# Sixteen slots instead of fourteen in an attention unit, and one VectorE operation less in the filler's gelu

## The chip, the cores and the metric

The kernel runs on one core of a Trainium2 chip. The metric is the device time of one execution in microseconds (us), median of three runs. A core has five engines with in-order queues of their own: TensorE (PE, with its weight loads listed as PEld), VectorE (DVE), ScalarE (ACT), GpSimd (POOL) and SyncE (SP), which issues the DMAs here.

## The reference

One transformer block in parallel form on x of 2048 tokens by 640 channels, float32:

```
xn = layernorm(x)
q, k, v = split(xn @ wqkv)              # 32 heads of 20 channels
s = (q k^T) / sqrt(20), kept where 0 <= i - j < 256, else -1e9
A = (softmax(s) @ v) @ wo               # sliding-window attention
B = (gelu_tanh(xn @ w_gate) * (xn @ w_up)) @ w_down     # 1728 hidden channels
out = x + A + B
```

The gelu is the tanh approximation: 0.5 g (1 + tanh(sqrt(2/pi) (g + 0.044715 g^3))).

## The kernel before

**Precision.** The dense products run in float32r with every operand split into a high and a low part (xh, xl for the normalized x; wqh, wql and so on for weights). A dense block of 128 rows by 512 tokens is then 3 x 5 = 15 matmuls: three combinations of parts, five slices of the 640 channels (dense_steps, L82). Queries and keys are stored as three bf16 parts in HBM and loaded as a stack, so that one matmul of 120 rows gives scores of float32 quality.

**Stages.** From 0 to 64 us: layernorm, transposes, first projections. From 64 to 714 us: the attention stage, into which the rest of the q, k and v projections and the gate and up products of eight of the fourteen column blocks of the gated layer are woven. From 714 us on: the remaining gate and up products, then w_down and wo and the sum.

**The attention stage.** A *unit* is one group of four heads and one chunk of 512 queries: 8 groups x 4 chunks = 32 units (NU). What a unit needs:

- 16 *maxima* (max_piece, L410 and L412): for one head and one block of 128 queries the scores against up to 384 keys, one or two bf16 matmuls into a bank of ps_m, and one VectorE operation that adds the mask and takes the row maximum. Chunk 0 has narrower ones (128, 256, 384, 384 columns). There are three ps_m banks (psm, L109). When a unit's sixteenth maximum is queued, two VectorE operations (L417, L418) negate the maxima and split them in two bf16 parts (nm).
- max_end (L424 to L427): one matmul turns nm around into ps_n, which takes a bank of the same three; ACT copies it (mr), a DMA puts it as two more rows under the queries' stack. With them the scores of the second pass come out less their maximum.
- 12 *exponentials* (exp_piece, L462 and L464): bf16 matmuls over 122 rows into one of two banks of ps_e, then Exp on ACT into the tile P; behind every fourth of them GpSimd cuts the diagonal (L470, L473).
- av_unit (L484): P times v in float32, 32 or 48 short matmuls into ps_o, a copy (ob) and DMAs.

The maxima run ahead of the exponentials: 24 of them are done before unit 0 starts, so while unit u takes its exponentials, maxima 8 to 15 of unit u+1 and 0 to 7 of unit u+2 are taken.

**Slots.** The order on TensorE, ACT and VectorE is the program's order (manual_schedule). attention() lays a unit out in NS = 14 *slots*. Slot 0 first takes av_unit of the unit before. Every even slot is a *cluster*: in slots 0 to 10 two exponentials, then two maxima, three of them in slots 6 and 12. After that every slot pulls RATE/NS = 3.54 matmuls from *filler()*, a generator over the dense work (ps_d, ps_v; ps_v counts 0.65). A max_end is due MXD = 4 slots after the slot of its sixteenth maximum.

Work that follows a dense block is not queued at once: defer(n, fn) puts it n slots later, and tick() at a slot's head queues what is due, ahead of that slot's exponentials and maxima. gate_up_fill has the chain c1 (ACT: copy gs and Square, L528, L529), c2 (VectorE, L534 and L535), c3 (ACT: Tanh, L539), c4 (VectorE, L543), one slot apart, and c5 (VectorE, L550, and a store to HBM) a slot after the up product. A q or k block has upper (ACT conversion L215, VectorE difference r L216) and lower (ACT conversion L203, GpSimd, DMAs). The split of the next weights puts a conversion on ACT (L510). x_sums queues 80 VectorE additions (L613, eight sets of ten, two slots apart, the first at slot XS0, sets XSN slots apart) for a later stage. The second half of v is projected when the slot number has reached V1_SLOT.

load_stack (L390) issues the six DMAs of a unit's queries and keys two units ahead, at slot 0.

Before unit 0 there is a ramp of twelve steps, each with two single maxima and 4 filler matmuls behind each, and then GAP = 16 of filler.

Of the kernel before, what the change touches and what calls it, by code (L numbers as in the profile page):

```python
# [12 lines left out]
AF = mybir.ActivationFunctionType  # L13
OP = mybir.AluOpType
# [12 lines left out]
SCALE = 1.0 / math.sqrt(DH)  # L27
NEG = -3.0e38
QROWS = 122
NS = 14  # L30
RATE = 49.6
V1_SLOT = 169
MXD = 4
NFA = 8
NDA = 2
WARM = 64
XS0, XSN = 24, 50
RAMP = 4.0
GAP = 16
VW = 1408  # L40
# [5 lines left out]
def block_kernel(ctx, tc, x, xt, wqk, wv, wo, wgu, wd, wdl, out):  # L46
    nc = tc.nc
# [30 lines left out]
    def dense_steps(ps, wh, wl, rh, rl, nk, cost=1.0):  # L78
        n = 0
        for a, b in ((wh, rh), (wl, rh), (wh, rl)):  # L80
            for k in range(nk):
                nc.tensor.matmul(ps, a(k), b(k), start=n == 0, stop=n == 3 * nk - 1)  # L82
                n += 1
                yield cost
# [84 lines left out]
    now = [None]  # L169

    def at(slot, fn, *a):
        acts.setdefault(slot, []).append((fn, a))

    def defer(n, fn, *a):
        if now[0] is None:
            fn(*a)
        else:
            at(now[0] + n, fn, *a)
# [94 lines left out]
    def run(*gens):  # L273
        for gen in gens:
            for _ in gen:
                pass
# [105 lines left out]
    def load_stack(u):  # L382
        g, c = divmod(u, NC)
        for m in range(80 * g // 128, (80 * g + 79) // 128 + 1):
            assert (m, c) in done and (m + 5, c) in done, (u, m)

        for dst, src, parts in ((qs[u % NQ], qd[c], (0, 1, 2)), (ks[u % NK], kd[c], (0, 0, 0))):
            slot = 0
            for part, n in zip(parts, (3, 2, 1)):
                nc.sync.dma_start(dst[DH * slot:DH * (slot + n)].rearrange("p j t -> p (j t)"),  # L390
                                  src[g, part:part + n].rearrange("s (d j) t -> (s d) (j t)", j=4))
                slot += n
# [3 lines left out]
    def max_piece(u, i):  # L396
        g, c = divmod(u, NC)
        j, b = divmod(i, 4)
        q, k = qs[u % NQ], ks[u % NK]
        if i == 0:  # L400
            maxes[u] = ap.tile([128, 4, 4], F32, name="mx", tag="mx")
        ps = psm.tile([128, 384], F32, name="ps_m", tag="mx")
        lh = q[0:120, j, 128 * b:128 * b + 128]
        old = max(0, 256 - 128 * b) if c else 0
        n0 = max(0, 128 * b - 256)
        n = old + 128 * b + 128 - n0
        parts = [(0, old, ks[(u - 1) % NK][0:120, j, C - old:C])] if old else []
        parts.append((old, n, k[0:120, j, n0:128 * b + 128]))
        for lo, hi, rhs in sorted(parts, key=lambda p: p[1] - p[0]):
            nc.tensor.matmul(ps[:, lo:hi], lh, rhs, start=True, stop=True)  # L410
        junk = ap.tile([128, 384], BF, name="junk", tag="junk", bufs=1)
        nc.vector.tensor_tensor_reduce(out=junk[:, 0:n], in0=ps[:, 0:n], in1=mask[:, 384 - n:384], scale=1.0,  # L412
                                       scalar=NEG, op0=OP.add, op1=OP.max, accum_out=maxes[u][:, j, b:b + 1])
        if i == 15:
            mx = maxes.pop(u)
            nm = nms[u % 2]
            nc.vector.tensor_scalar(nm[:, 0, 0], mx, -1.0, None, op0=OP.mult)  # L417
            nc.vector.scalar_tensor_tensor(nm[:, 0, 1], mx, -1.0, nm[:, 0, 0], op0=OP.mult, op1=OP.subtract)  # L418
            maxes[u] = nm
# [85 lines left out]
    def split_later(pool, bufs, raw):  # L505
        hi = pool.tile([128, KT, 128], F32R, name="wqh", tag="wqh", bufs=bufs)
        lo = pool.tile([128, KT, 128], F32R, name="wql", tag="wql", bufs=bufs)

        def high():
            nc.scalar.activation(hi, raw, AF.Copy)  # L510
            for k in range(KT):
                defer(1 + k, low, k)

        def low(k):
            nc.gpsimd.tensor_tensor(out=lo[:, k], in0=raw[:, k], in1=hi[:, k].bitcast(F32), op=OP.subtract)  # L515

        defer(1, high)
        return hi, lo

    def gate_up_fill(f, ws, c):  # L520
        cs = slice(c * C, (c + 1) * C)
        pss = []
        st = {}

        def c1():
            gs = st["g"] = hp.tile([128, C], F32, name="gs", tag="gs")
            t = st["t"] = hp.tile([128, C], F32, name="he", tag="he", bufs=2)
            nc.scalar.activation(gs, pss[0], AF.Copy)  # L528
            nc.scalar.activation(t, pss[0], AF.Square)  # L529
            defer(1, c2)  # L530

        def c2():
            gs, t = st["g"], st["t"]
            nc.vector.tensor_scalar(t, t, 0.044715, 1.0, op0=OP.mult, op1=OP.add)  # L534
            nc.vector.tensor_tensor(out=t, in0=gs, in1=t, op=OP.mult)  # L535
            defer(1, c3)

        def c3():
            nc.scalar.activation(st["t"], st["t"], AF.Tanh, scale=math.sqrt(2.0 / math.pi))  # L539
            defer(1, c4)  # L540

        def c4():
            nc.vector.scalar_tensor_tensor(st["g"], st["t"], 1.0, st["g"], op0=OP.add, op1=OP.mult)  # L543
            st["done"] = True

        def c5():
            if "done" not in st:
                defer(1, c5)
                return
            nc.vector.scalar_tensor_tensor(st["t"], st["g"], 0.5, pss[1], op0=OP.mult, op1=OP.mult)  # L550
            nc.sync.dma_start(hd[f][c], st["t"])

        for i, (wh, wl) in enumerate(ws):
            ps = psd.tile([128, C], F32, name="ps_d", tag="dn")
            pss.append(ps)
            yield from dense_steps(ps, lambda k: wh[:, k, :], lambda k: wl[:, k, :],
                                   lambda k: xh[:, k, cs], lambda k: xl[:, k, cs], KT)
            defer(1, c5 if i else c1)
# [6 lines left out]
    def filler():  # L565
# [6 lines left out]
        for s, (kind, i) in enumerate(sets[:-1]):  # L572
            nxt = []
            after = sets[s + 1]
            for c in range(NC):
# [14 lines left out]
                if c in (1, 2) and c <= len(raws):  # L590
                    nxt.append(split_later(*pools[(s + 1) % 2], raws[c - 1]))
                if pending and now[0] >= V1_SLOT:
                    pending = False
# [65 lines left out]
    def pull_max(n, slot):  # L659
        for _ in range(n):  # L660
            x = next(stream, None)
            if x is None:
                return
            max_piece(*x)
            if x[1] == 15:
                at(slot + MXD, max_end, x[0])

    def tick():
        return [y for t in sorted(t for t in acts if t <= now[0]) for y in acts.pop(t)]

    def pull_fill(n):
        debt[0] += n
        while debt[0] > 0:
            debt[0] -= next(fill, 1.0)

    def attention():
        now[0] = -1
        load_stack(0)
        load_stack(1)
        load_stack(2)  # L680
        for i, (p, k, half) in enumerate((p, k, half) for p in range(NC // 2) for k in range(2) for half in range(2)):
            for j, fn in enumerate(x_sums(p, k, half)):
                at(XS0 + XSN * i + 2 * j, fn)
        for i in range(12):
            now[0] = i - 13
            for fn, a in tick():
                fn(*a)
            for _ in range(2):
                pull_max(1, now[0])
                pull_fill(RAMP)  # L690
        pull_fill(GAP)
        for u in range(NU + 1):
            if 1 <= u and u + 2 < NU:
                load_stack(u + 2)
            for i in range(NS):
                T = now[0] = NS * u + i
                for fn, a in tick():
                    fn(*a)
                if i == 0 and u:
                    av_unit(u - 1)  # L700
                if i % 2 == 0:
                    if u < NU and i < 12:
                        exp_piece(u, i)
                        exp_piece(u, i + 1)
                    pull_max(3 if i in (6, 12) else 2, T)
                pull_fill(RATE / NS)
        while acts:
            now[0] += 1
            for fn, a in tick():
                fn(*a)  # L710
        now[0] = None
        run(fill)
        assert not acts

    with tc.manual_schedule(engines=MANUAL):
        attention()
# [363 lines left out]
    for n, (c, kind, i) in enumerate(steps):  # L1080
        if (kind, i) == ("d", 0):
            pss = [psn.tile([128, C], F32, name="ps_w", tag="w") for _ in range(KT)]
# [57 lines left out]
```

## Time and profile before

| | |
|---|---|
| median of 3 runs | 1117.17 us (1116.29 to 1118.18) |
| the profiled execution | 1116.69 us, span 1115.0 us |
| mean granted TensorE clock | 0.995 |
| TensorE busy | 1098.7 us, 6802 matmuls |
| VectorE busy | 637.7 us, 1736 operations |
| ACT busy | 470.9 us, 952 operations |
| GpSimd busy | 359.9 us, 504 operations |
| HBM traffic | 118 GB/s over the span |
| attention stage, 92 to 714 us | TensorE busy 617.1 of 622.0 us, VectorE 420.5, ACT 329.1 |

In the groups of instructions a row has line, engine, operation, tile written and read, shapes and count, then the busy time and the mean duration in ns of one, then idle time of the engine ahead of it and who ended it. In the timeline a row has start and length in us, engine, line, operation, tiles, shape and count of a merged run of equal instructions, and in brackets the idle time of the engine ahead. In the windows a row has the stretch, its length, then busy time and count for PE, PEld, DVE, ACT and POOL, then TensorE's clock, the DMA share and GB/s. Matmuls overlap, and their ends are modelled: the distance from one start to the next tells more of TensorE than the durations.

### The profile page before, as it was taken

The numbers are of one execution on the slowest core, as the hardware profiler recorded it, in microseconds if no ns is written. First come the engines' busy times: TensorE is split into PE (matmuls) and PEld (weight loads), VectorE is DVE, ScalarE is ACT, GpSimd is POOL, SyncE is SP. The second block draws the span as 40 slices with busy tenths as digits, with TensorE's granted clock in tenths as the row PEclk, the third lists the DMA queues.
The fourth block names the chain that finished last, engine by engine and source line by source line (L and its number), as shares of the span: only waits on it lengthen the run. The fifth ranks groups of instructions, "written<-read, shape, count | busy, mean of one in ns | idle before, by whom it ended". The sixth has DMA issues, their size and how long they took to land.

```text
span 1115.0 us, 19319 instructions
## 1 busy us (share of the span) xinstructions
PE 1098.7 (99%) x6802; PEld 837.6 (75%) x6802; DVE 637.7 (57%) x1736; ACT 470.9 (42%) x952; POOL 359.9 (32%) x504
## 2 busy tenths in 40 slices
PE   7999999999999999999999999999999999999998
PEld 7887666767668876667667676788888878788886
DVE  7856676757648577586777775566664350211203
ACT  4434554555555455645545454643323421211111
POOL 4122542644552233534323343311113313222230
PEclk8999999999999999999999999999999999999999
DMA  4642343543443314343242431342214835152431
GB/s 157 220 143 60 103 144 115 139 146 95 139 144 109 87 58 143 111 146 107 80 140 83 125 104 38 107 150 92 89 66 157 264 125 175 48 179 75 152 95 66
DMA packets 76145, 133.10 MB, mean 119 GB/s; under 512 B 12800, under 2 KB 33664, under 8 KB 76048
## 3 DMA queue, kind: packets, MB, share of 16 engines
q1 hardware_dynamic: 76048, 131.87, 37.6%
q8 instruction: 53, 0.87, 0.3%
q14 instruction: 44, 0.36, 0.1%
HBM read 86.31 MB, written 44.83 MB: 118 GB/s over the span
## 4 chain that ended last, share of the span: by engine, by line
PE 91%; DVE 4%; ACT 1%; DMA 1%; issue 1%; POOL 1%; SPq 0%; DVEq 0%; ACTq 0%; POOLq 0%
PE ps_d L82 28%; PE ps_w L942 23%; PE ps_g L851 11%; PE ps_o L484 7%; PE ps_e L462 7%; PE ps_m L410 6%; PE ps_v L82 6%; DVE junk L412 2%; PE ps_g L82 1%; PE ps_t L156 1%; PE ps_d L296 1%; ACT P L464 1%; PE ps_b L912 0%; DMA xi<-x 0%; DMA qs<-qd 0%
## 5 line engine op out<-in xcount | busy, mean ns | idle before, releaser
L412 DVE CUSTOM_DVE_ANT_0 junk<-ps_m,mask 128x384 bf16<-128x384 f32 (+2 forms) x512 | 271.2, 530 | 158.0 <-PE ps_m L410 120.0
L464 ACT ACTIVATE P<-ps_e 128x512 f32<-128x512 f32 (+2 forms) x384 | 197.5, 568 | 71.0 <-PE ps_e L462 64.6
L470 POOL TENSOR_SCALAR_AFFINE_SELECT P<-P 128x512 f32<-128x512 f32 x128 | 83.8, 655 | 221.1 <-ACT P L464 212.8
L82 PE MATMUL ps_d<-xh,wqh 128*128 128x512 f32 x510 | 150.4, 407 | 0.0
L82 PE MATMUL ps_d<-xh,wql 128*128 128x512 f32 x510 | 150.3, 407 | 0.0
L82 PE MATMUL ps_d<-xl,wqh 128*128 128x512 f32 x510 | 149.3, 406 | 0.0
L410 PE MATMUL ps_m<-ks,qs 120*128 120x128 bf16 (+1 forms) x704 | 120.9, 275 | 4.1 <-DVE mx L412 2.8
L921 POOL TENSOR_TENSOR ht<-hr,ht 128x512 fp32r<-128x512 f32 x52 | 69.2, 1337 | 172.1 <-ACT ht L919 142.9
L462 PE MATMUL ps_e<-qs,ks 122*128 122x128 bf16 (+2 forms) x704 | 112.5, 277 | 0.8 <-ACT P L464 0.6
L82 PEld LDWEIGHTS ps_d<-xl,wqh 128*128 128x128 f32 x510 | 92.9, 188 | 19.2 <-issue 2.4
L82 PEld LDWEIGHTS ps_d<-xh,wql 128*128 128x128 f32 x510 | 93.1, 189 | 18.0 <-issue 0.9
L82 PEld LDWEIGHTS ps_d<-xh,wqh 128*128 128x128 f32 x510 | 92.6, 188 | 17.2 <-ACT xh L164 0.3
L919 ACT ACTIVATE ht<-hr 128x512 fp32r<-128x512 f32 x56 | 35.1, 629 | 132.7 <-PE ps_w L942 80.8
L462 PEld LDWEIGHTS <-ks 122*128 122x128 bf16 x704 | 49.9, 98 | 54.6 <-issue 44.3
L473 POOL TENSOR_SCALAR_AFFINE_SELECT P<-P 128x512 f32<-128x512 f32 x112 | 74.2, 673 | 51.2 <-ACT P L464 51.2
L410 PEld LDWEIGHTS <-qs 120*128 120x128 bf16 x704 | 62.1, 98 | 33.1 <-issue 13.7
L484 PE MATMUL ps_o<-P,v 128*32 128x384 f32 (+2 forms) x1408 | 84.3, 386 | 0.0
L204 POOL TENSOR_TENSOR pt<-r,pt 128x512 bf16<-128x512 f32 x40 | 47.3, 1181 | 105.1 <-ACT pt L203 104.8
L484 PEld LDWEIGHTS ps_o<-P,v 128*32 128x32 f32 x1408 | 40.1, 110 | 39.6 <-issue 32.8
L923 DVE TENSOR_TENSOR ht<-hr,ht 64x512 fp32r<-64x512 f32 x4 | 2.8, 690 | 112.3 <-ACT ht L919 112.3
L515 POOL TENSOR_TENSOR wql<-wr,wqh 128x128 fp32r<-128x128 f32 x115 | 51.6, 481 | 38.0 <-ACT wqh L510 38.0
L488 ACT ACTIVATE ob<-ps_o 128x512 f32<-128x512 f32 x32 | 19.1, 597 | 101.1 <-PE ps_o L484 58.5
(270 smaller groups left out, 1889.2 us busy)
## 6 DMA issues: line engine op xcount, KB each, us to landing
hd<-he SPq DMA_DIRECT2D x52, 256.0 KB
hr<-hd SPq DMA_DIRECT2D x52, 256.0 KB
wr<-wgu SPq DMA_DIRECT2D x27, 320.0 KB
qs<-qd SPq DMA_DIRECT2D x32, 240.0 KB
ks<-kd SPq DMA_DIRECT2D x32, 240.0 KB
xi<-x SPq DMA_DIRECT2D x16, 320.0 KB
qs<-qd SPq DMA_DIRECT2D x32, 160.0 KB
ks<-kd SPq DMA_DIRECT2D x32, 160.0 KB
```

The source lines that it names most:

```text
L82: nc.tensor.matmul(ps, a(k), b(k), start=n == 0, stop=n == 3 * nk - 1)
L410: nc.tensor.matmul(ps[:, lo:hi], lh, rhs, start=True, stop=True)
L412: nc.vector.tensor_tensor_reduce(out=junk[:, 0:n], in0=ps[:, 0:n], in1=mask[:, 384 - n:384], scale=1.0, scalar=NEG, op0=OP.add, op1=OP.max ...
L462: nc.tensor.matmul(ps[:, col:col + n], k[0:QROWS, j, kc:kc + 128], q[0:QROWS, j, q0:q0 + n], start=True, stop=True)
L464: nc.scalar.activation(pt[:, j, lo:hi], ps[:, lo:hi], AF.Exp, scale=SCALE)
L470: nc.gpsimd.affine_select(out=a, in_=a, pattern=[[0, 4], [1, 128]], compare_op=OP.is_ge, fill=0.0, base=0, channel_multiplier=-1)
L473: nc.gpsimd.affine_select(out=a, in_=a, pattern=[[0, 4], [-1, 128]], compare_op=OP.is_ge, fill=0.0, base=-1, channel_multiplier=1)
L484: nc.tensor.matmul(o[32 * j:32 * j + 32, q0:q0 + n], v[:, w0_:w0_ + 32], pt[:, j, col:col + n], start=i == 0, stop=i == len(todo) - 1, ski ...
L515: nc.gpsimd.tensor_tensor(out=lo[:, k], in0=raw[:, k], in1=hi[:, k].bitcast(F32), op=OP.subtract)
L851: nc.tensor.matmul(ps, i, j, start=first and n == 0, stop=n == len(work) - 1, skip_group_check=True)
L921: nc.gpsimd.tensor_tensor(out=t[:, 1, :], in0=raw, in1=t[:, 0, :].bitcast(F32), op=OP.subtract)
L942: nc.tensor.matmul(pss[m], w[:, ms], r, start=first and j == 0, stop=last and j == len(work) - 1)
```

## The change

Two things. A unit has 16 slots, in eight clusters with two maxima each; the constants that count slots are set anew (V1_SLOT, MXD, XS0, XSN), RATE per unit stays, and the ramp ends at slot -3, with two more slots of GAP/2 filler each behind it, whose due work is queued at their heads. And the polynomial of the gelu takes one VectorE operation instead of two: the factor 0.044715 goes into ACT's Square as its scale, and (t + 1) g is one scalar_tensor_tensor.

```diff
-NS = 14
+NS = 16
 RATE = 49.6
-V1_SLOT = 169
-MXD = 4
+V1_SLOT = 193
+MXD = 5
...
-XS0, XSN = 24, 50
+XS0, XSN = 28, 57
 RAMP = 4.0
 GAP = 16
...
             nc.scalar.activation(gs, pss[0], AF.Copy)
-            nc.scalar.activation(t, pss[0], AF.Square)
+            nc.scalar.activation(t, pss[0], AF.Square, scale=math.sqrt(0.044715))
             defer(1, c2)
...
             gs, t = st["g"], st["t"]
-            nc.vector.tensor_scalar(t, t, 0.044715, 1.0, op0=OP.mult, op1=OP.add)
-            nc.vector.tensor_tensor(out=t, in0=gs, in1=t, op=OP.mult)
+            nc.vector.scalar_tensor_tensor(t, t, 1.0, gs, op0=OP.add, op1=OP.mult)
             defer(1, c3)
...
         for i in range(12):
-            now[0] = i - 13
+            now[0] = i - 14
             for fn, a in tick():
                 fn(*a)
             for _ in range(2):
                 pull_max(1, now[0])
                 pull_fill(RAMP)
-        pull_fill(GAP)
+        for i in (-2, -1):
+            now[0] = i
+            for fn, a in tick():
+                fn(*a)
+            pull_fill(GAP / 2)
...
-                    pull_max(3 if i in (6, 12) else 2, T)
+                    pull_max(2, T)
                 pull_fill(RATE / NS)
```

## The prediction

> **What bounds the kernel now.** I read the busy times first, then the windows by stage, then who waited for whom in the attention stage, then the timeline of TensorE (PE) around the waits.
>
> ```profile
> PE 1098.7 (99%) x6802; PEld 837.6 (75%) x6802; DVE 637.7 (57%) x1736; ACT 470.9 (42%) x952; POOL 359.9 (32%) x504
> ```
> ```profile
> 92.00:714.00 622.00, 617.09 (x4530) 440.02 (x4529) 420.46 (x1318) 329.11 (x675) 247.52 (x399) 1.00 0.36 109
> ```
>
> TensorE is busy for 99% of the span, and in the attention stage (92 to 714 us, the only one the diff touches) for 617.1 of 622.0 us at clock 1.00. The matmuls are the same before and after, so the change can only move two things: time in which TensorE waits, and what its switches between float32 filler and bf16 pieces cost. VectorE (DVE) is busy for 420 us of that stage, so its own saving is worth what TensorE waits for it, no more.
>
> ```profile
> PE ps_m L410 <- DVE mx L412: 2.8, 8, 0.4
> PE ps_m L410 <- DMA sd<-ob: 0.6, 1, 0.6
> PE ps_e L462 <- ACT P L464: 0.6, 1, 0.6
> PE ps_m L410 <- DMA od<-ob: 0.3, 1, 0.3
> ```
>
> These waits hold 4.3 us, but they count from the modelled end of the matmul ahead. The timeline shows more:
>
> ```profile
> 160.84 0.66 PE L410 MATMUL ps_m<-ks,qs 120*128 120x384 bf16 x4
> ...
> 166.02 0.32 PE L410 MATMUL ps_m<-ks,qs 120*128 120x384 bf16 x1
> 166.73 0.33 PE L410 MATMUL ps_m<-ks,qs 120*128 120x128 bf16 x2 [0.39 <-DVE mx L412]
> ```
>
> The second row starts 0.71 us before the third, where a 384-wide bf16 matmul takes 0.16: a stall of 0.55. I did this for every TensorE start of the stage (distance to the next start, less the median of the same pair of shapes, where over 15 ns): **9.1 us of stall**, by slot of the unit 1.6 in slot 6, 4.8 in slot 10, 2.6 in slot 12 and 0.1 before the first unit. Slots 6 and 12 hold the threes; slot 10 comes four to five maxima after slot 6. By unit u of the loop: units 9, 12, 20, 23 (x-sums and gelu together) 3.1; units 1, 18, 29 (an exponential's bank not free, ACT late) 1.5; the rest 4.5, of which 1.25 in units 2 and 11 is the unit's first maximum waiting for its loads (the two DMA rows: issued at 309.8 to 312.1 in unit 11, the wait ends at 317.1).
>
> Why VectorE is late:
>
> ```profile
> 163.52 0.54 DVE L412 CUSTOM_DVE_ANT_0 junk<-ps_m,mask 128x384 bf16<-128x384 f32 x1
> ...
> 163.99 0.70 DVE L543 SCALAR_TENSOR_TENSOR gs<-he,gs 128x512 f32<-128x512 f32 x1
> 164.80 0.69 DVE L550 SCALAR_TENSOR_TENSOR he<-gs,ps_d 128x512 f32<-128x512 f32 x1
> 165.41 0.55 DVE L412 CUSTOM_DVE_ANT_0 junk<-ps_m,mask 128x384 bf16<-128x384 f32 x1
> ...
> 166.11 0.56 DVE L412 CUSTOM_DVE_ANT_0 junk<-ps_m,mask 128x384 bf16<-128x384 f32 x1
> ```
>
> Its queue is in order. From start to start a maximum costs 0.71 ahead of another (0.48 ahead of other work), an elementwise operation on 512 columns 0.60; its bank is free 0.62 after its start (166.11 to 166.73).
>
> **The change, part by part.** Sums are against the profiled execution, 1116.69 us (span 1115.0 and 1.7 around it), 0.48 below the median of 1117.17.
>
> *The gelu operation.* L534 goes: 32 x 0.457 (its start to the next start) = 14.6 us off VectorE. The operation left has two tensors like L535, rows 0.69 to 0.75, and L543 of the new form has 0.71: no difference. ACT's Square takes the factor as its scale, no instruction more. None of the 14.6 is on TensorE's path by itself; it counts in the queue below.
>
> *Sixteen slots.* The filler per unit stays 49.6, so 6.2 matmuls of 0.2275 us stand between clusters instead of 7.09. A cluster with four ps_e comes every 2.36 us (155.57 to 157.93), then every 2.18; the two without exponentials every 1.74. The units take as long as before.
>
> *Clusters: one more a unit.* A cluster costs its own widths and a switch: the first float32 matmul behind it takes 0.314 to 0.319 (behind 256 columns) or 0.367 (behind 384) instead of 0.2275, the last bf16 one 0.027 instead of its 0.11 or 0.16, the matmul ahead 0.003 more: 0.008 to 0.013 net. Thirty more: +0.3.
>
> *ps_n alone.* MXD 5 puts max_end at slot 6 + 5 = 11, an odd slot with no cluster; before it opened the cluster of slot 10 and cost 0.066. Alone a 128-wide one costs what the ramp shows:
>
> ```profile
> 69.69 0.39 PE L82 MATMUL ps_d<-xh,wqh 128*128 128x512 f32 x1
> 69.92 0.23 PE L410 MATMUL ps_m<-ks,qs 120*128 120x128 bf16 x1
> 69.96 1.17 PE L82 MATMUL ps_d<-xh,wqh 128*128 128x512 f32 x4
> 70.97 0.28 PE L410 MATMUL ps_m<-ks,qs 120*128 120x256 bf16 x1
> ```
>
> From 69.92 to 70.97 there are 1.05 us for it and four matmuls of 0.2275: 0.13 to 0.14, 0.07 more than in a cluster. 32 x 0.064 = +2.0.
> What gives a little back: before, a cluster ended 14 times on a 128-wide maximum (odd counts, chunk 0), at 0.06 a switch; pairs always end on 256 or 384: -0.7. **Order of TensorE: +1.6**, from 0.8 (half the price alone) to 2.4.
>
> The Trainium skill's page "TensorE: Matmul & The Clock Gate" (Step-by-step: what each phase is for) says that weight loads are pulled ahead of matmuls in flight, so that the next weights load while this tile streams. By that the switches are free and this term is 0; the rows above (1.05 us, not 0.97) disagree.
>
> *The stalls.* I wrote down which operations each slot queues on VectorE and ACT after the change (from defer, at and the pulls) and added row durations from the first maximum of slot 6 on. The tight place: ps_n of slot 11 takes one of the three psm banks, so the second maximum of slot 12 needs the second of slot 10. In an idle queue that is started 0.81 + 0.71 into slot 10 and released at 2.14; TensorE wants it at 2.18 + 0.12 + 0.16 = 2.46. 0.3 us to spare (0.2 where the exponentials are narrow, chunk 0).
> Unit 9, from the start of slot 6: the gelu product until 1.04 (its Square is ready at 0.43), maxima 14 and 15 until 2.35, two negations (0.23 + 0.47) 3.05, x-sum 0.36 and L543 0.60 4.01, maxima 0 and 1 5.20, x-sum and L550 6.16, maximum 2 6.87, maximum 3 free at 7.49. TensorE: 3 x 2.18 + 0.28 = 6.82. Stall 0.7. For unit 4 of before the same addition gives 0.5, and the trace has 0.54.
> So for all units:
> - 9, 12, 20, 23 (x-sums and gelu): 0.7, 1.2, 0.9, 0.5 = 3.3, against 3.1.
> - 1, 11, 19, 26, 29: a conversion or Tanh stands ahead of slot 8's exponentials on ACT and waits for a VectorE operation behind the negations (done 3.4 into slot 6); exponentials and so slot 10's ps_e are late by 0.45 each: 2.3. Before, 1.5 in 1, 18, 29.
> - 2, 16: Square behind mr at slot 11, the product ahead of slot 12's maxima: 0.2 each. 6, 21, 24, 27: 0.1 each. 0.8.
> - The first maximum of a unit comes in slot 8, 2.73 + 4 x 2.18 + 0.44 = 11.9 us into it, and in unit 11 the loads were there after 11.1: the 1.25 goes.
> - The other 3.2 of threes goes: the load from slot 6 to 10 is one maximum (0.71) less.
> Sum 6.4 instead of 9.1, **-2.7**. Bounds 2.5 (only the work itself too long in those four units) and 11 (the tight place missed by 0.15 us in every unit).
>
> *Moved, at nothing.* ps_n to the exponentials of its unit: 0.7 + 2 x 1.74 + 2.73 = 6.9 us for mr (0.27), SP and a DMA whose packets end 1.5 to 2.5 after issue; SP was late by up to 3.0 (mr ended 554.6, issue 557.5). In the ramp 23 filler matmuls (3.4 us) cover 2.5. Selects on POOL have 5.7 us to the AV pass, 4.6 before. x-sums and V1_SLOT keep their place in units (28/16 for 24/14; 193/16 for 169/14). Without that cover each costs its lateness, some 0.5 us a unit.
>
> **Sum**: 1116.69 + 1.6 - 2.7 = 1115.6 for a run like the profiled one; with 0.5, 1116.1.
>
> **Rivals.**
> (1) *The queue runs dry* (faster): slot 6's burst was the root, and stalls fall to 2.5. For it: 7 of 9.1 us lie in slots 10 and 12, behind it. Against: four units carry more VectorE work than the stretch has time. 2.5 - 9.1 + 1.6 = -5.0: 1112.2.
> (2) *The bank of ps_n at slot 12* (slower): 0.2 to 0.3 us to spare is less than one elementwise operation. If in some twenty units where I forecast nothing one lands in that stretch, 0.3 each: stalls 12.4, +3.3 + 1.6 = +4.9: 1122.1. It decides from 0.30 us of stall a unit on (9.7 in all; my sum is 0.2 a unit). For it: before, the same bank one slot earlier cost 4.8 us. Against: VectorE idles 0.8 us between slots 8 and 10.
> (3) *The switches are hidden*: what a lone ps_n adds is overlapped by weight loads that run ahead, and the +1.6 falls away: 1114.5. The ramp rows speak against it. This is the rule of the Trainium skill's page "TensorE: Matmul & The Clock Gate" named above.
>
> **Numbers.** A measurement of this kernel can tell about 0.2%, 2.2 us, from no change. My sum, within that: 0.48. Rival 1: 0.27, rival 3: 0.04, both faster: 0.31. Rival 2: 0.21. Time 1116.1; the likeliest case alone spans 1114.3 to 1118.5 (stalls 5 to 8, order 1.2 to 2.0). The range goes to rival 1 and to most of rival 2: 1112.0 to 1121.0.
>
> **What would show it.** ps_n alone between ps_d rows, 32 times, first matmul behind it at 0.31; stalls in slot 12's second ps_m and slot 10's ps_e, none at a unit's first maximum; L534 gone, VectorE 14 to 15 us less busy. Wrong if the stage (92 to 714) is over 2 us shorter or longer, or if TensorE stalls where no maximum or exponential is due.

## The result, and the profile after

The changed kernel takes 1119.88 us (median of 10 runs, 1119.52 to 1120.83) against 1117.28 for the kernel before, measured with it: ratio 1.0027, 95% interval 1.0017 to 1.0036. It is slower by about 2.6 us where 1.1 less was forecast. The profiled execution took 1120.12 us, span 1118.4.

From the page, the busy times of the kernel after; then the window of the attention stage (columns as before):

```profile
PE 1100.4 (98%) x6802; PEld 831.6 (74%) x6802; DVE 626.5 (56%) x1704; ACT 472.8 (42%) x952; POOL 361.6 (32%) x504
```
```profile
92.00:714.00 622.00, 616.12 (x4484) 432.90 (x4487) 407.04 (x1283) 331.08 (x676) 248.16 (x399) 1.00 0.36 109
```

VectorE has 32 operations and 11.2 us less. TensorE has the same 6802 matmuls, but by 714 us it has done 46 fewer of the stage's (4484 against 4530): the stage got longer. Who waited for whom, of the rows that belong to this stage:

```profile
PE ps_e L462 <- ACT P L464: 3.1, 7, 0.9
...
PE ps_m L410 <- DVE mx L412: 1.6, 2, 0.9
```

Both rows have turned round. VectorE's maxima held TensorE 8 times for 2.8 us and now hold it twice for 1.6; the exponentials on ACT, once for 0.6, now seven times for 3.1. The rows with a DMA are gone.

To compare kernels I measured the stage from the first ps_m to the last ps_o, and in it the stalls as the prediction does (start to start, beyond what the same pair of shapes usually takes), now with the ramp's first clusters and the first instruction of each cluster. Before: 648.9 us, of it 9.6 stalls, and 639.3 without them. After: 652.0, 11.2 and 640.8. So of 3.2 us more, **1.5 are the order of TensorE and 1.6 are stalls**. By what stalled: ps_m 7.3 before and 2.9 after, ps_e 1.8 and 7.0.

### The profile page after: what moved, and what is told of

It reads as the page before. It is cut to its first block, busy times and chain, and to the rows that moved or that the text cites. A ratio compares the mean times of both kernels' runs of the same rounds, so it can differ in the third digit from the quotient of the medians.

```text
span 1118.4 us, 19302 instructions
## 1 busy us (share of the span) xinstructions
PE 1100.4 (98%) x6802; PEld 831.6 (74%) x6802; DVE 626.5 (56%) x1704; ACT 472.8 (42%) x952; POOL 361.6 (32%) x504
## 4 chain that ended last, share of the span: by engine, by line
PE 90%; DVE 4%; issue 3%; ACT 1%; POOL 1%; DMA 1%; SPq 0%; DVEq 0%; POOLq 0%; ACTq 0%
PE ps_d L82 28%; PE ps_w L945 22%; PE ps_g L854 11%; PE ps_o L484 7%; PE ps_e L462 7%; PE ps_m L410 7%; PE ps_v L82 5%; PE ps_g L82 1%; DVE junk L412 1%; ACT P L464 1%; PE ps_t L156 1%; PE ps_d L296 1%; POOL pt L204 0%; DVE r L216 0%; DMA xi<-x 0%
## 5 line engine op out<-in xcount | busy, mean ns | idle before, releaser
L470 POOL TENSOR_SCALAR_AFFINE_SELECT P<-P 128x512 f32<-128x512 f32 x128 | 85.9, 671 | 232.5 <-ACT P L464 224.3
L82 PE MATMUL ps_d<-xh,wqh 128*128 128x512 f32 x510 | 153.5, 410 | 0.0
L82 PE MATMUL ps_d<-xh,wql 128*128 128x512 f32 x510 | 153.0, 410 | 0.0
L82 PE MATMUL ps_d<-xl,wqh 128*128 128x512 f32 x510 | 152.9, 410 | 0.0
L410 PE MATMUL ps_m<-ks,qs 120*128 120x128 bf16 (+1 forms) x704 | 124.2, 276 | 1.8 <-DVE mx L412 1.6
L82 PEld LDWEIGHTS ps_d<-xl,wqh 128*128 128x128 f32 x510 | 92.3, 189 | 17.7 <-issue 1.5
L473 POOL TENSOR_SCALAR_AFFINE_SELECT P<-P 128x512 f32<-128x512 f32 x112 | 74.5, 675 | 41.5 <-ACT P L464 35.8
```

Source lines behind the costliest of these rows:

```text
L470: nc.gpsimd.affine_select(out=a, in_=a, pattern=[[0, 4], [1, 128]], compare_op=OP.is_ge, fill=0.0, base=0, channel_multiplier=-1)
L473: nc.gpsimd.affine_select(out=a, in_=a, pattern=[[0, 4], [-1, 128]], compare_op=OP.is_ge, fill=0.0, base=-1, channel_multiplier=1)
```

## Where the stalls come from: one unit read closely

Unit 26 after the change, slots 6 to 10, from the timelines of VectorE, GpSimd, ACT and TensorE:

```profile
610.90 0.56 DVE L412 CUSTOM_DVE_ANT_0 junk<-ps_m,mask 128x384 bf16<-128x384 f32 x1
...
611.50 0.48 DVE L417 TENSOR_SCALAR nm<-mx 128x16 bf16<-128x16 f32 x1
612.01 0.55 DVE L418 SCALAR_TENSOR_TENSOR nm<-mx,nm 128x16 bf16<-128x16 f32 x1
612.49 0.68 DVE L534 SCALAR_TENSOR_TENSOR he<-he,gs 128x512 f32<-128x512 f32 x1
...
611.32 0.64 POOL L470 TENSOR_SCALAR_AFFINE_SELECT P<-P 128x512 f32<-128x512 f32 x1 [2.29 <-ACT P L464]
611.90 0.64 POOL L473 TENSOR_SCALAR_AFFINE_SELECT P<-P 128x512 f32<-128x512 f32 x1
612.49 1.17 POOL L470 TENSOR_SCALAR_AFFINE_SELECT P<-P 128x512 f32<-128x512 f32 x1
...
610.09 1.10 ACT L464 ACTIVATE P<-ps_e 128x512 f32<-128x512 f32 x2
613.20 0.63 ACT L538 ACTIVATE he<-he 128x512 f32<-128x512 f32 x1 [2.01 <-DVE he L534]
613.74 2.13 ACT L464 ACTIVATE P<-ps_e 128x512 f32<-128x512 f32 x4
...
611.52 0.61 PE L462 MATMUL ps_e<-qs,ks 122*128 122x256 bf16 x4
...
612.60 1.08 PE L82 MATMUL ps_d<-xl,wqh 128*128 128x512 f32 x4
614.37 0.86 PE L462 MATMUL ps_e<-qs,ks 122*128 122x256 bf16 x4 [0.69 <-ACT P L464]
```

Read it from the end. The ps_e of slot 10 should start 4 x 0.2275 behind 612.60, at 613.51, and starts at 614.37: no bank of ps_e is free. The banks hold slot 8's scores (TensorE wrote them from 611.52 on), whose exponentials start at 613.74 only. They stand behind the Tanh L538, which tick() queued at the head of slot 8, and the Tanh had ACT idle for 2.01 us, waiting for the gelu product L534. The product stands behind the two negations, which take 0.99 us (611.50 to 612.49). Then the second ps_e pays again: its bank comes free one exponential later (0.53), and TensorE would be there in 0.22, so its row is 0.86 long instead of 0.61. The whole stall is 1.11 us; the waits row shows 0.69 of it.

The same chain, with a Tanh or with the conversion L203 behind r (L216), stalls slot 10's ps_e in seven units: 1, 11, 12, 19, 23, 26 and 29 with 1.13, 0.62, 1.18, 0.62, 0.72, 1.11 and 0.61 us, 6.0 together. Before it was three units.

## The experiments

Two theories were to be told apart. **The chain**: what costs is negations, VectorE operation and Tanh or conversion in front of slot 8's exponentials; the number of units in which a dense block ends at that phase decides, not sixteen slots as such. **The order**: sixteen slots cost through the lone ps_n and its bank. All runs are timed against the kernel before in the same runs; its own median was between 1116.3 and 1117.4 us in them, so a difference of two times below is good to about 1 us.

**Each half alone: the gelu with fourteen slots (e1), sixteen slots with the old gelu (e2).**

```diff
 # e1, from the kernel before
-            nc.scalar.activation(t, pss[0], AF.Square)
+            nc.scalar.activation(t, pss[0], AF.Square, scale=math.sqrt(0.044715))
...
-            nc.vector.tensor_scalar(t, t, 0.044715, 1.0, op0=OP.mult, op1=OP.add)
-            nc.vector.tensor_tensor(out=t, in0=gs, in1=t, op=OP.mult)
+            nc.vector.scalar_tensor_tensor(t, t, 1.0, gs, op0=OP.add, op1=OP.mult)
 # e2: the same lines the other way, from the kernel after
```

> The kernel before with only the gelu's operation taken out, fourteen slots kept. Theory A (what the change lost, it lost by its slots; VectorE time in front of a maximum or of a Tanh is worth what TensorE waits there): the stalls of before in units with gelu (2, 3, 4, 9, 12, 16, 20, 23, 29; 5 us) shrink by up to 0.46 each, so 1114 to 1115.5 us, stalls 6 to 7 us instead of 9.6. Theory B (VectorE is not the limit anywhere, only the order on TensorE counts): 1117.3, no change.

> The changed kernel with the two old gelu operations, so the slots alone. Theory A: in units 12, 23, 26 and 29 the Tanh ahead of slot 8's exponentials comes 0.46 us later, in units 9, 16 and 20 the maxima do: 1.5 to 3 us above the changed kernel, 1121.4 to 1123. Theory B: as the changed kernel, 1119.9.

e1: 1113.83 us, ratio 0.9973 [0.9964, 0.9983]; stalls 6.9. e2: 1126.14 us, ratio 1.0082 [1.0068, 1.0096]; stalls 17.7, of them 12.4 in ps_e. The waits of e2:

```profile
PE ps_e L462 <- ACT P L464: 6.4, 9, 1.5
```

Taking one gelu operation away is worth about 3.5 us of time with fourteen slots and 6.3 with sixteen (1126.14 to 1119.88). The prediction gave it nothing of its own beside the queue. It stands in the chain: in unit 26 the ps_e stall is 1.9 us in e2 and 1.1 in the change. The slots alone cost 8.9 us with the old gelu and 6.0 with the new one.

**ps_n in a cluster (e3): sixteen slots, MXD 4.** It is then due at slot 10, heads that cluster, and no longer stands alone in slot 11.

```diff
-MXD = 5
+MXD = 4
```

> The changed kernel with MXD 4, so that ps_n stands at the head of slot 10's cluster instead of alone in slot 11. Both theories: the switch of a lone ps_n goes, 32 x 0.064 = 2.0 us. Theory A: the stalls in front of slot 10's ps_e stay (the chain is the same, 5 to 6 us), those at slot 12 go, 0.2 to 1.2 us: 1117 to 1118. Theory B (the order on TensorE is the loss): 1116.5 or less, more than the 2.0.

1118.24 us, ratio 1.0007 [0.9998, 1.0016]. The stage without its stalls falls from 640.8 to 639.2 us, which is that of fourteen slots (639.3): the order's cost is this instruction, 1.7 us. Stalls stay (11.7). So the order is one half of the loss and cannot be the other.

**The Tanh out of the way (e4).** A Tanh, or a lower step of q or k (the conversion L203 and what follows it), that is due at slot 8 is queued at slot 9, behind slot 8's exponentials.

```diff
+    def past_8():
+        return 2 if now[0] is not None and (now[0] + 1) % NS == 8 else 1
...
-            defer(1, lower)
+            defer(past_8(), lower)
...
-            defer(1, c3)
+            defer(past_8(), c3)
```

> The changed kernel; a Tanh or a conversion of q/k (the lower step) that falls due at slot 8 is queued at slot 9 instead, behind slot 8's exponentials. Seven units are touched (1, 11, 12, 19, 23, 26, 29), with 6.0 us of stall at slot 10's ps_e among them. Theory A (these two stand ahead of the exponentials on ACT and wait for a VectorE operation behind the negations): the 6.0 us go, some 0.5 to 1 us comes back at slots 10 to 12, so 1114.5 to 1115.5. Theory B: 1119.9, since the waits only move.

1116.34 us, ratio 0.9989 [0.9981, 0.9998]: 3.5 us less than the change. The ps_e stalls go from 7.0 to 1.0, in all seven units at once; those of ps_m rise from 2.9 to 5.7, 1.7 of it in unit 12 at slot 12:

```profile
PE ps_m L413 <- DVE mx L415: 3.6, 5, 1.6
```

**The negations out of the way (e6).** L417 and L418 are queued three slots later, at slot 9; ps_n at slot 11 is what needs them.

```diff
-            nc.vector.tensor_scalar(nm[:, 0, 0], mx, -1.0, None, op0=OP.mult)
-            nc.vector.scalar_tensor_tensor(nm[:, 0, 1], mx, -1.0, nm[:, 0, 0], op0=OP.mult, op1=OP.subtract)
+            def negate():
+                nc.vector.tensor_scalar(nm[:, 0, 0], mx, -1.0, None, op0=OP.mult)
+                nc.vector.scalar_tensor_tensor(nm[:, 0, 1], mx, -1.0, nm[:, 0, 0], op0=OP.mult, op1=OP.subtract)
+
+            defer(3, negate)
```

> The changed kernel; the two negations of a unit's maxima (L417, L418) are queued at slot 9 instead of directly behind the sixteenth maximum in slot 6. Theory A (the Tanh or conversion of slot 8 is late because its VectorE operation of slot 7 stands behind the negations): that operation is ready 0.7 to 1.0 us earlier, and the 6 us at slot 10's ps_e fall to 1 or less, as in the kernel where Tanh and conversion stand behind the exponentials; the negations now stand ahead of slot 10's maxima and cost up to 0.3 us at slot 12 in some ten units, 1 to 3 us: 1115 to 1118. Theory C (the negations don't matter, it is only the place of the Tanh on ACT): 1119 to 1120.

1113.14 us, ratio 0.9968 [0.9957, 0.9980]: 6.7 us less than the change, with nothing removed. Unit 26 in its timelines (VectorE, ACT, TensorE):

```profile
605.62 0.56 DVE L412 CUSTOM_DVE_ANT_0 junk<-ps_m,mask 128x384 bf16<-128x384 f32 x1
...
606.10 1.11 DVE L538 SCALAR_TENSOR_TENSOR he<-he,gs 128x512 f32<-128x512 f32 x1
...
607.91 0.41 DVE L419 TENSOR_SCALAR nm<-mx 128x16 bf16<-128x16 f32 x1
608.36 0.18 DVE L420 SCALAR_TENSOR_TENSOR nm<-mx,nm 128x16 bf16<-128x16 f32 x1
...
607.24 0.63 ACT L542 ACTIVATE he<-he 128x512 f32<-128x512 f32 x1 [1.34 <-DVE he L538]
...
608.41 0.87 PE L466 MATMUL ps_e<-qs,ks 122*128 122x256 bf16 x4
```

The product starts 0.48 us behind the unit's last maximum instead of 1.59, and the Tanh 1.62 behind it instead of 2.30, although the product itself takes 1.11 here. The stall in this unit is 0.44 instead of 1.11; over all units stalls are 5.0 (ps_m 1.2, ps_e 2.1, and 0.9 once where ps_n waits for its negations). In slot 10 the ps_e stalls fall from 6.0 to 1.0. The stage without stalls stays at 640.9. So the chain starts at the negations: with the Tanh left where it was, moving them takes most of it away.

**The phase alone (e7, e8).** GAP shifts every dense block against the slots by two matmuls, with the same work and slots. Counted in the program's order, a Tanh or conversion is due at slot 8 in 2 units with sixteen slots and GAP 18 (7 in the change), and in 7 units with fourteen slots and GAP 14 (3 before).

```diff
 # e7, from the kernel after
-GAP = 16
+GAP = 18
 # e8, from the kernel before
-GAP = 16
+GAP = 14
```

> The changed kernel with GAP 18 instead of 16: two filler matmuls more before unit 0, so that every dense block ends two matmuls earlier against the slots. By the order of the program a Tanh or q/k conversion then falls due at slot 8 in two units (1 and 29) instead of seven. Theory A': the sixteen slots lost because of where the filler's blocks end against slot 8, not by being sixteen: stalls at slot 10's ps_e 1.5 to 2 us instead of 6, time 1115 to 1117. Rival D (sixteen slots leave too little time between clusters, wherever the blocks end): 1119 to 1121.

> The kernel before (fourteen slots, old gelu) with GAP 14 instead of 16: a Tanh or q/k conversion falls due at slot 8 in seven units (1, 11, 12, 19, 23, 26, 29) instead of three. Theory A': stalls at the ps_e behind slot 8 rise from 1.8 to 5 to 8 us, other places fall by 1 to 3: 1119 to 1123. Rival D: fourteen slots have the time: 1117 to 1118.

e7: 1116.85 us, ratio 0.9998 [0.9989, 1.0007], stalls 8.1, ps_e 3.0. e8: 1121.11 us, ratio 1.0038 [1.0025, 1.0052], stalls 13.0, ps_e 5.3. With the old gelu and seven units in that phase, fourteen slots (e8) take 1121.1 and sixteen (e2) 1126.1: of the 8.9 us that sixteen slots seemed to cost, 3.8 are the phase. With the new gelu the phase is 3.0 (e7) of 6.0. So about half of it is where the filler's blocks happen to end. The other half is not the lone ps_n's 1.7 alone, and the first theory was too strong: with the same seven units and the old gelu, slot 10's ps_e stall for 4.4 us with fourteen slots (e8, in five of the seven) and for 8.5 with sixteen (e2, in all seven), so sixteen slots also raise the price of a unit in that phase. Why they do was not measured. GAP moves every other block too, so these two runs are a test of the phase as a whole and not of slot 8 alone.

**Fourteen slots with the new gelu and the Tanh moved (e9).** The edits of e1 and e4 together.

> Fourteen slots with the new gelu, and a Tanh or lower step due at slot 8 queued at slot 9. Theory A: in units 1, 18 and 29 the 1.0 us at slot 10's ps_e goes; 1112.5 to 1113.5, at or up to 1 us below the kernel with the gelu alone (1113.83).

1112.91 us, ratio 0.9971 [0.9960, 0.9983]. Against e1 the ps_e stalls go from 1.1 to 0 and the time falls by 0.9, less than the intervals tell apart: with three units in that phase there is less to win.

**Negations and ps_n moved (e10; e11 the same with fourteen slots and the new gelu).** MXD 6 lets ps_n head slot 12's cluster.

```diff
 # e10, from the kernel after, with the edit of e6
-MXD = 5
+MXD = 6
 # e11, from e1, with the edit of e6
-MXD = 4
+MXD = 6
```

> The change, with the two negations (L417, L418) queued three slots after a unit's sixteenth maximum, at slot 9, and with max_end due six slots after it instead of five (MXD 6), so that ps_n heads the cluster of slot 12 instead of standing alone in slot 11. Theory (the slow time is made of two parts that add: a lone ps_n, 1.7 us by the pair of MXD 5 and 4, and a chain from the negations over ACT to ps_e of slot 10, gone when the negations stand behind): the order of TensorE is back at that of fourteen slots, 639.2 us of the attention stage without stalls, stalls stay at about 5 us as in the kernel with the negations moved alone, so 1113.1 - 1.7 = 1111.4 us. Rival (ps_n at slot 12 takes the bank that the maxima of that cluster wait for, and leaves mr and its DMA 4.5 us only ahead of the exponentials): stalls rise by 2 us or more, 1113 to 1118 us, with ps_m waits in slot 12 or a wait of ps_e in slot 0 for the DMA.

> Fourteen slots with the new gelu, with the two negations queued at slot 9 instead of in the slot of the sixteenth maximum (6) and max_end due at slot 12 (MXD 6), where ps_n heads a cluster as it does at slot 10 before. Theory (negations ahead of the gelu product and the differences delay ACT's exponentials whatever the number of slots): of the 6.9 us of stalls that fourteen slots with the new gelu have, those behind slot 8 (1.1 us in ps_e) and a part of those of slot 10's maxima go, and 1111 to 1113 us come out against 1113.8. Rival (with fourteen slots the stalls belong to the threes of slots 6 and 12, and the negations matter only where sixteen slots put seven units in the bad phase): no change, 1113.8 within 0.8, or worse through ps_n at slot 12 ahead of three maxima.

e10: 1116.58 us, ratio 1.0002 [0.9993, 1.0011]. The order is back at 639.1 us, 1.8 below e6, a second measure of the lone ps_n; but stalls rise from 5.0 to 10.8, 5.7 of them in slot 12, as its rival had it; one ps_e in slot 0 waits for mr's DMA (0.4), which the rival named too. One of those in slot 12, in unit 2 (timeline of TensorE):

```profile
147.46 0.23 PE L428 MATMUL ps_n<-identb,nm 128*128 128x128 bf16 x1
148.04 0.33 PE L410 MATMUL ps_m<-ks,qs 120*128 120x128 bf16 x2 [0.36 <-ACT mr L430]
```

The maximum behind ps_n waits until ACT has copied ps_n out, a stall of 0.52. e11 is worse: 1122.41 us, ratio 1.0049 [1.0035, 1.0063]. Its stage takes 655.6 us. There slot 12 has three maxima behind ps_n, and it stalls in nearly every unit (some 8.6 us in all), and twice a unit's first ps_e waits for mr's DMA (3.3 us). Both theories of moving ps_n into slot 12 fell: standing alone in slot 11 it costs 1.7 us, and that buys an empty cluster.

**The negations alone, with fourteen slots (e12).** e11 with MXD 4, so that ps_n stays at slot 10, and only the negations have moved.

> Fourteen slots with the new gelu and the negations queued at slot 9; max_end stays at slot 10 (MXD 4), so that ps_n keeps its place and the bank of slot 12 is free as before. Only the two negations have moved. Theory (the negations' delay matters through the phase in which ACT's chain falls due at slot 8, which at fourteen slots three units have): of 6.9 us of stalls 1 to 1.5 go, the ones of ps_e in slot 10 and some of slot 10's maxima: 1112.3 to 1113.0 us. Rival (the negations now stand in front of slot 10's maxima, or leave max_end too little time): ps_m or ps_n stalls in slot 10 rise by what is saved, 1113.8 us or above.

1120.89 us, ratio 1.0039 [1.0027, 1.0052], some 7 us above e1. The theory fell, the rival holds. The waits, and unit 19 in the timelines of VectorE, GpSimd and TensorE:

```profile
PE ps_n L428 <- DVE nm L420: 7.3, 11, 1.3
```
```profile
478.29 0.60 DVE L419 TENSOR_SCALAR nm<-mx 128x16 bf16<-128x16 f32 x1
478.92 1.08 DVE L420 SCALAR_TENSOR_TENSOR nm<-mx,nm 128x16 bf16<-128x16 f32 x1
...
478.83 1.15 POOL L204 TENSOR_TENSOR pt<-r,pt 128x512 bf16<-128x512 f32 x1
...
478.39 0.39 PE L82 MATMUL ps_d<-xh,wqh 128*128 128x512 f32 x1
480.07 0.23 PE L428 MATMUL ps_n<-identb,nm 128*128 128x128 bf16 x1 [1.29 <-DVE nm L420]
```

Queued one slot ahead of ps_n, the negations are late for it, 10.4 us in all; two slots ahead, in e6, it was 0.9. The move that gains 6.7 us with sixteen slots loses 7 with fourteen, because of where ps_n stands. So it is the room between the negations and ps_n that decides, and the slot of its own for ps_n gave that room; fourteen slots with ps_n moved to slot 11 were not run.

**Both moves (e13).** The edits of e4 and e6 on the change.

> The change with both moves: negations at slot 9, and a Tanh or conversion due at slot 8 queued at slot 9. Theory: both take away the same chain, so they don't add: with the negations moved 5.0 us of stalls are left, of which 0.4 (unit 26) and perhaps unit 12's 0.5 are of that chain. 1112.2 to 1113.2 us, no faster than fourteen slots with the second move alone (1112.9), since the lone ps_n's 1.7 us stay. Rival (separate delays on different engines, so that the gains of 6.7 and 3.5 us add): 1110 us.

1113.07 us, ratio 0.9964 [0.9951, 0.9978], stalls 4.5. The two moves take away the same chain: 3.5 and 6.7 us alone, 6.8 together.

| kernel | ratio to before | stage, us | stalls: all (ps_m, ps_e, ps_n) | stage less stalls |
|---|---|---|---|---|
| before | | 648.9 | 9.6 (7.3, 1.8, 0) | 639.3 |
| after | 1.0027 | 652.0 | 11.2 (2.9, 7.0, 0) | 640.8 |
| e1 gelu, 14 slots | 0.9973 | 646.3 | 6.9 (5.4, 1.1, 0) | 639.4 |
| e2 old gelu, 16 slots | 1.0082 | 658.6 | 17.7 (4.1, 12.4, 0) | 640.9 |
| e3 after, MXD 4 | 1.0007 | 650.9 | 11.7 (4.1, 6.4, 0.4) | 639.2 |
| e4 after, Tanh moved | 0.9989 | 648.9 | 8.0 (5.7, 1.0, 0) | 640.9 |
| e6 after, negations moved | 0.9968 | 645.9 | 5.0 (1.2, 2.1, 0.9) | 640.9 |
| e7 after, GAP 18 | 0.9998 | 649.4 | 8.1 (3.6, 3.0, 0) | 641.3 |
| e8 before, GAP 14 | 1.0038 | 651.8 | 13.0 (6.9, 5.3, 0) | 638.8 |
| e9 e1, Tanh moved | 0.9971 | 644.4 | 5.1 (4.7, 0, 0) | 639.2 |
| e10 e6, MXD 6 | 1.0002 | 649.9 | 10.8 (7.3, 2.5, 0.2) | 639.1 |
| e12 e1, negations moved | 1.0039 | 653.1 | 13.8 (3.0, 0, 10.4) | 639.2 |
| e13 e4 and e6 | 0.9964 | 645.4 | 4.5 (1.8, 1.0, 0.9) | 641.0 |

The rest of the stalls are those of ps_d and ps_v; e11 is left out. Six kernels share 640.8 to 641.3 less stalls, and what sets them apart from the 638.8 to 639.4 of the others is the lone ps_n. Four kernels (e1, e6, e9, e13) beat the one before by 0.3%; their intervals overlap.

## Why the prediction was wrong, point by point

**The order of TensorE, forecast +1.6: right.** It is +1.5 (639.3 to 640.8). (The prediction's own line for what it gives back, 14 switches at 0.06, makes 0.8 and not the 0.7 it used: 1.5 in all.) ps_n stands alone 32 times, and its terms hold: the matmul behind it starts its successor after 0.31 us. Unit 26:

```profile
616.11 0.23 PE L424 MATMUL ps_n<-identb,nm 128*128 128x128 bf16 x1
616.15 0.94 PE L82 MATMUL ps_d<-xh,wqh 128*128 128x512 f32 x3
616.93 0.34 PE L410 MATMUL ps_m<-ks,qs 120*128 120x128 bf16 x2
```

0.82 us for it and three matmuls of 0.2275 leave 0.14. Over 32 units it costs 1.7 or 1.8 (e3, e10) where the ramp's row gave 2.0. With it the rival of hidden switches falls, and with it the reading that weight loads pulled ahead make a switch free, by the rule that the Trainium skill's page "TensorE: Matmul & The Clock Gate" gives.

**The stalls, forecast 9.1 to 6.4: wrong, and this step turned the sign.** They went from 9.6 to 11.2. Term by term:

| units | forecast, us | measured, us |
|---|---|---|
| 9, 12, 20, 23 (x-sums and gelu) | 3.3 | 0.2 + 1.5 + 1.1 + 0.7 = 3.5 |
| 1, 11, 19, 26, 29 (conversion or Tanh ahead of slot 8's exponentials) | 5 x 0.45 = 2.3 | 4.1 |
| 2, 16; 6, 21, 24, 27 | 0.8 | 1.6, of it unit 16 1.0 |
| units forecast at nothing | 0 | 0.8 (5, 7, 13, 14) |
| before unit 1 | 0 | 1.2, of it 0.4 in the ramp's first clusters, as before; 0.8 in GAP and unit 0's first clusters |

The mechanism of the second row was named with its units, and all five are there. What was mis-sized is its price, "late by 0.45 each". In unit 26 it is 1.11 = 0.45 + 0.39 + 0.27. The 0.39: the product was done 3.79 us into slot 6 (609.38 to 613.17), not 3.4, of which 0.29 is that the negations took 0.99 where the sum had 0.23 + 0.47, a middle value of a row that is spread widely. The 0.27: only the first of slot 10's two ps_e was charged; the second pays one exponential more in every unit of the row (units 11, 19 and 29 are 0.35 + 0.27). The first row's total came out right by luck: in units 12 and 23 most of the stall is ps_e in slot 10, the chain again, and not ps_m in slot 12, and in unit 9, which the prediction worked out at 0.7, it is 0.2 (that sum charges 1.31 us for maxima 14 and 15, where its own prices, 0.71 and 0.48, make 1.19). In unit 16 an x-sum took 0.92 instead of 0.42, and one maximum stalled 1.0.

Of the 4.8 us between 6.4 and 11.2, then, 1.8 are the price of that row, 0.8 are unit 16, 0.8 units forecast at nothing, and 1.2 lie before unit 1, of which 0.4 had been left out of the count before as well. With the row at its measured 4.1 and all else as forecast, the stalls would have fallen by 0.9 and not by 2.7, less than the order's 1.6: the sign turns on this row. The 0.8 in GAP and unit 0's first clusters stand in no term of the sum. By the rows it is a chain of the same kind (ACT, VectorE):

```profile
94.90 0.63 ACT L203 ACTIVATE pt<-r 128x512 bf16<-128x512 f32 x1 [1.53 <-DVE r L216]
...
94.17 0.69 DVE L216 TENSOR_TENSOR r<-ps_d,pt 128x512 f32<-128x512 f32 x1 [2.50 <-POOL pt L204]
```

The difference r waits until GpSimd has read the r before it. A ps_v matmul starts at 94.92, once r is done, and behind the conversion, which ends at 95.53, ACT's copies of ps_v and the first Exp come late. In the kernel before, the conversion of that block stood behind the first exponentials. No run moved it, so this cause is read from the rows and not shown.

What was said of VectorE held as far as it went: ps_m stalls fell by 4.4, at a unit's first maximum nothing waits any more, and the loads' 1.25 are gone. The tally before had shown the other wait too, 1.5 us in units 1, 18 and 29, but it was carried on as a small term and not counted again for the phase that sixteen slots would set.

**"None of the 14.6 is on TensorE's path by itself": wrong as a price.** By e1 it is 3.5 us, by e2 6.3. VectorE was busy 11.2 us less, not 14 to 15: L534 had held 14.7, and L542 and the negations took 1.6 and 1.7 more.

**The rivals.** The slower one (ps_n's bank at slot 12) has the sign and not the place: slot 12's cluster stalls 1.4 us in the change, nearly all in three units, not 0.3 in some twenty. Of the 4.8 us that spoke for it, 1.5 were ps_e by the prediction's own tally and so not that bank. Its mechanism is real one slot on, in e10 and e11. The queue did not run dry: the lowest stalls of any kernel here are 4.5 us (e13), against 2.5 in that rival.

**What was to show it.** The stage is 3.2 us longer, over the bound of 2 that was set as the mark of a wrong sum. (The likeliest case had a slip too: stalls of 8 and an order of 2.0 give 1118.1, not 1118.5.)

## What to carry to other kernels

When slots or constants shift, list for each unit which deferred operation heads which slot, and follow it over two engines: an ACT operation that waits for VectorE holds every exponential queued behind it, and TensorE pays for each bank of the pair. Cost such a chain by the long end of each row's spread and charge all instructions behind the wait, not the first alone. A small operation off the bound engine (two negations of 16 columns) was worth 6.7 us here by its place alone; before a layout is blamed, shift the phase (GAP) of the old one too.

## What the runs showed of the hardware

The negations take longer when GpSimd works beside them. L418 has two inputs in SBUF; it takes 0.18 us (23 units of e6, with GpSimd idle, 0.174 to 0.177) and 0.55 in the median of the change, where in 31 of 32 units a GpSimd operation runs beside it. Unit 26 above shows the turns: the negations end at 611.98 and 612.56, just behind the selects' 611.96 and 612.54, and then the third select, begun with L534 at 612.49, takes 1.17 instead of 0.64. Both negations together hold VectorE for 26.6 us in the change and 16.5 in e6, so their move also made them shorter. L549, which has one of its two inputs in PSUM, isn't touched: it takes 0.68 in the median beside GpSimd and away from it. The Trainium skill's page "SBUF — State Buffer", section "Who interferes with whom", says that a VectorE instruction with two SBUF inputs contends with a GpSimd instruction that reads SBUF, and that the port pair they share is an exclusive lock; these rows agree. The rows are of kernels made for other questions; a run with GpSimd's selects moved and all else kept wasn't made, so how much of the 6.7 us this is stays open.
